# Linear attention and SiLU feed-forward on one core: opening outputs of each half of the heads in PSUM banks of their own, w_in loaded in 512-KB pieces through the pair ring, and two chunks' transposes issued ahead of later loads

## The chip, the cores and the metric

The kernel runs on one core of a Trainium2 chip. The metric is the device time of one execution in microseconds (us), lower is better. Each kernel was run several times, and medians are quoted with their range. The span, which the profile uses, is a little shorter than the device time: 212.7 us of 214.42 for the profiled run of the kernel before. The engines are called as the profile calls them: PE is the TensorE matmul, PEld its weight load, DVE is VectorE, ACT is ScalarE, POOL is GpSimd, and SP is the engine that issues the DMAs, whose queue appears as SPq.

## The reference

The computation has two parts. A causal linear attention with decay runs over 4 batches, 8 heads, 768 positions and head dimension 64. Its output, 3072 tokens of width 512, goes through a feed-forward network (FFN) with a SiLU.

```python
for b in range(nb):                                   # blocks of 64 positions
    sl = slice(b * block, (b + 1) * block)
    qb, kb, vb = (q[:, :, sl], k[:, :, sl], v[:, :, sl])
    intra = np.einsum('bhic,bhjc->bhij', qb, kb) * Dmask[None]
    intra = np.einsum('bhij,bhjd->bhid', intra, vb)
    inter = np.einsum('bhid,bhde->bhie', qb * lam_pow[None], kv_state)
    out[:, :, sl] = intra + inter
    kv_state = lam_block * kv_state + np.einsum('bhsd,bhse->bhde', kb * rev_pow, vb)
# ...
x = attn_out.transpose(0, 2, 1, 3).reshape(3072, 512)
h = x @ w_in                                          # 512 x 2048
out = (h / (1 + np.exp(-h))) @ w_out                  # 2048 x 512
```

## The kernel before

The kernel works in chunks of 128 tokens, 24 in all. Chunks are joined to groups of 256 or 384 tokens for the FFN. While the FFN of one group runs on the PE, the attention of the next group is woven in between. The start is special: chunks 0 to 3 (two pairs, "the opening") are written as an explicit list of small operations, because the PE has nothing else to do until weights have arrived.

For later chunks, POOL scales q and k (tiles `qb` and `kb`), SP issues a DMA transpose of each (`qt` and `kn`), and DVE spreads `kn` into a zero-padded tile `ktbd` (I call these the K copies). Only then can the PE compute the chunk's scores (`sp`).

Everything that SP issues, loads, transposes and stores, goes out in one order:

```python
def dma_t(c):
    qb, kb, vb = natb[c]
    # ... (tiles qt, kn)
    nc.sync.dma_start_transpose(qt, qb.rearrange("s p j d -> s (p j d)"))
    nc.sync.dma_start_transpose(kn, kb.rearrange("s p j d -> s (p j d)"))

def next_prep():
    c = state["prepped"]
    if c < NCHUNK:
        prep(c)                       # POOL: qb, kb
        if c >= NPET:
            dma_t(c)
        state["prepped"] = c + 1
        if loads:
            load_c(loads.pop(0))      # q, k, v of a later chunk, 256 KB each
# ... after the first groups' down-projections:
    st_d(5)
    next_prep()
    down0(3, 0)
    st_o(5)
    next_prep()
    clear_halves(0, 1)                # POOL: four memsets of ktbd and vpad
    down0(3, 1)
```

The opening leaves the tokens of groups 0 and 1 in a permuted order. Before the change a tile of 128 results holds every second token of the 256. The store of these four tiles therefore goes to every second row of the output:

```python
# op_x: attention outputs to the FFN's input, columns in the order (r, x, w)
move(e, xt[g].rearrange("d p (r x w) -> d p r x w", r=2, x=2)[:, ps, :, x, :], op_[c][:, ps])
# ...
# ffn2: result tile ob, 128 x 512
dst = out[r0:r0 + BLK, :]
if g < 2:
    dst = out[gstart[g]:gstart[g] + 256, :].rearrange("(q r) d -> q r d", r=2)[:, mt, :]
stores.append([0, dst, ob])           # issued later by nc.sync.dma_start(out=dst, in_=ob)
```

w_in is loaded in sixteen pieces of 256 KB into buffers that nothing else uses yet, and w_out in eight pieces of 512 KB through a ring of six buffers called `pair`. Each piece is then cast to bf16.

## Time and profile before

| what | before |
|---|---|
| time, median of 3 (range) | 215.58 us (214.94 to 215.84) |
| span of the profiled run | 212.7 us |
| PE busy | 204.5 us, 96% |
| first down-projection of the FFN | 33.59 us |
| longest PE wait after 22 us | 0.94 us, chunk 7's scores |

The first fence is from the page of the kernel before: the busy times of its first part, then busy tenths in 40 slices of 5.3 us each, the granted PE clock (the speed at which the PE was let run) in tenths of full speed (9 is 90% or more), and the DMA's share and rate.

```profile
PE 204.5 (96%) x1808; PEld 136.0 (64%) x1831; DVE 112.2 (53%) x263; ACT 98.4 (46%) x186; POOL 54.3 (26%) x66
...
PE   7979999999899999999999999999999999999994
...
PEclk9999999999999999999999999999999999999999
DMA  4999999998999997897999999889311011011112
GB/s 125 332 375 340 396 401 309 291 225 214 160 266 203 231 199 164 168 220 165 206 222 246 222 196 172 192 214 196 99 52 49 2 49 54 0 49 49 52 49 99
```

The PE is full except in the first slices. The DMA engines are over 90% busy from the second slice to the ninth and stay near it while chunks are being loaded, so the DMA has little slack either. The PE row counts 1808 matmuls and the PEld row 1831 weight loads. The records of 23 matmuls are missing from this trace.

The second fence is the view of the PE's waits before the change. Its columns are the total in us, how often, and the longest.

```profile
PE warm_ps L646 <- DVE zero L118: 1.1, 1, 1.1
PE sp L476 <- DVE ktbd L183: 0.9, 1, 0.9
PE kv_ps L641 <- ACT kvbd L179: 0.9, 1, 0.9
PE h_ps L529 <- ACT w_in_bf L179: 0.7, 1, 0.7
PE tk L270 <- POOL kp L253: 0.4, 1, 0.4
```

Only the 0.9 us for `ktbd` falls after the opening. The third fence is SP's timeline between 45 and 64 us, with start and length of each issue. `qt` and `kn` are the transposes of chunks 6, 7 and 8, and `out_dram<-ob` the stores.

```profile
46.93 1.21 SPq L374 DMA_TRANSPOSE kn<-kb  x1
...
50.61 1.18 SPq L570 DMA_DIRECT2D out_dram<-ob  x1
...
53.20 1.22 SPq L374 DMA_TRANSPOSE kn<-kb  x1
...
57.46 1.60 SPq L570 DMA_DIRECT2D out_dram<-ob  x3
59.23 1.24 SPq L373 DMA_TRANSPOSE qt<-qb  x1
60.56 1.21 SPq L374 DMA_TRANSPOSE kn<-kb  x1
61.82 0.57 SPq L232 DMA_DIRECT2D qf<-in_q_dram  x1
```

SP issues back to back.

The fourth fence is the view by windows of the kernel before. The columns are the window, its length, busy time (and count) of PE, PEld, DVE, ACT and POOL, granted clock, DMA share, and GB/s.

```profile
21.00:33.00 12.00, 11.54 (x106) 10.35 (x107) 5.81 (x12) 8.93 (x17) 0.00 (x0) 1.00 1.06 395
...
56.00:61.00 5.00, 4.00 (x45) 3.17 (x44) 3.67 (x10) 3.15 (x6) 2.14 (x2) 1.00 1.03 278
61.00:66.00 5.00, 5.00 (x38) 2.99 (x37) 2.63 (x9) 1.30 (x4) 0.60 (x1) 1.00 1.02 223
66.00:73.00 7.00, 6.95 (x76) 5.58 (x75) 4.51 (x11) 4.00 (x8) 3.03 (x4) 1.00 0.88 203
73.00:82.00 9.00, 8.90 (x94) 7.02 (x94) 7.48 (x18) 4.24 (x8) 2.70 (x3) 1.00 0.85 187
```

The last three permuted stores were issued from 57.46 us on and landed 3.6 to 3.7 us later. From 56 to 66 us, with other transfers in flight too, the DMA moves 278 and then 223 GB/s at a share of about 1, so on all of its 16 engines. (The share adds up the times of all packets, so it can pass 1; I read it only roughly.)

### The profile page before, as it was taken

Reading aid. Unit: us, or ns where it says so; the run is one execution under the profiler, and the core shown is the slowest. Engines: PE = TensorE matmul, PEld = TensorE weight load, DVE = VectorE, ACT = ScalarE, POOL = GpSimd, SP = SyncE. Lnnn points to the kernel's source line nnn. Section 1 sums busy time; section 2 is a strip of 40 time slices with the busy share of each in tenths; the row PEclk is TensorE's granted clock in tenths of the full one; section 3 lists DMA queues with packets and bytes.
Section 4 is the critical chain, followed back from the end, with each engine's and each line's share of the span. In section 5 each row is a group of like instructions: output and inputs, shape, how many; then the busy total and the mean of one; then the engine's idle time right before and its main releaser. Section 6 shows DMA issues by size and latency. Waiting matters only on the chain.

```text
span 212.7 us, 4591 instructions
## 1 busy us (share of the span) xinstructions
PE 204.5 (96%) x1808; PEld 136.0 (64%) x1831; DVE 112.2 (53%) x263; ACT 98.4 (46%) x186; POOL 54.3 (26%) x66
## 2 busy tenths in 40 slices
PE   7979999999899999999999999999999999999994
PEld 5667885567767877666665565556665565566654
DVE  3786458396766789555846975455561351110121
ACT  4983863415734554445554444444544344323210
POOL 6360004469333341313333432233000000000000
PEclk9999999999999999999999999999999999999999
DMA  4999999998999997897999999889311011011112
GB/s 125 332 375 340 396 401 309 291 225 214 160 266 203 231 199 164 168 220 165 206 222 246 222 196 172 192 214 196 99 52 49 2 49 54 0 49 49 52 49 99
DMA packets 95670, 38.58 MB, mean 181 GB/s; under 512 B 81056, under 2 KB 88608, under 8 KB 95648
## 3 DMA queue, kind: packets, MB, share of 16 engines
q1 hardware_dynamic: 95504, 38.29, 72.2%
q8 instruction: 14, 0.23, 0.5%
q14 instruction: 8, 0.07, 0.1%
q10 hardware_dynamic: 144, 0.00, 0.0%
HBM read 27.27 MB, written 6.29 MB: 158 GB/s over the span
## 4 chain that ended last, share of the span: by engine, by line
PE 71%; DMA 16%; SPq 9%; issue 1%; DVE 1%; POOL 1%; DVEq 0%
PE o_ps L578 30%; PE h_ps L552 20%; PE h_ps L529 11%; DMA pair<-in_moe_w_out_dram 4%; PE op L507 4%; SPq L224 4%; DMA qf<-in_q_dram 4%; SPq L232 3%; PE sp L476 3%; DMA vf<-in_moe_w_in_dram 3%; DMA qf<-in_moe_w_in_dram 3%; DMA kn<-kb 2%; PE o_part L595 2%; PE kv_ps L452 1%; SPq L161 1%
## 5 line engine op out<-in xcount | busy, mean ns | idle before, releaser
L578 PE MATMUL o_ps<-w_out_bf,g 128*128 128x512 bf16 x345 | 87.9, 379 | 1.2
L578 PEld LDWEIGHTS <-g 128*128 128x128 bf16 x368 | 35.0, 98 | 30.8
L556 ACT ACTIVATE g<-h_ps 128x384 bf16<-128x384 f32 x64 | 31.4, 490 | 46.7 <-PE h_ps L552 46.2
L552 PE MATMUL h_ps<-xt,w_in_bf 128*128 128x384 bf16 x256 | 50.6, 326 | 0.0
L529 PE MATMUL h_ps<-xt,w_in_bf 128*128 128x256 bf16 x384 | 47.2, 273 | 0.7 <-ACT w_in_bf L179 0.7
L534 ACT ACTIVATE g<-h_ps 128x512 bf16<-128x512 f32 x48 | 27.8, 596 | 32.4 <-PE h_ps L529 32.0
L529 PEld LDWEIGHTS <-w_in_bf 128*128 128x128 bf16 x384 | 36.4, 98 | 8.0 <-ACT w_in_bf L179 1.1
L582 DVE COPY ob<-o_ps 128x512 f32<-128x512 f32 x23 | 15.9, 691 | 41.1 <-PE o_ps L578 40.9
L356 POOL TENSOR_TENSOR qb<-qf,lam_fwd 128x512 bf16<-128x512 f32 x18 | 18.9, 1053 | 63.4 <-DMA qf<-in_q_dram 60.1
L552 PEld LDWEIGHTS <-w_in_bf 128*128 128x128 bf16 x256 | 23.7, 98 | 17.2
L483 DVE TENSOR_TENSOR ss<-sp,mask 128x512 bf16<-128x512 f32 (+1 forms) x40 | 21.0, 566 | 13.4 <-PE sp L476 13.0
L387 DVE COPY vpad<-vb 64x256 bf16<-64x256 bf16 x72 | 24.9, 346 | 1.6
L350 POOL TENSOR_TENSOR kb<-kf,lam_bwd 128x512 bf16<-128x512 f32 x20 | 21.7, 1086 | 4.4 <-DMA kf<-in_k_dram 4.0
L183 DVE CAST kvbd<-kv_ps 64x256 bf16<-64x256 f32 x32 | 13.5, 421 | 8.2 <-PE kv_ps L452 7.9
L515 ACT ACTIVATE xt<-op 128x512 bf16<-128x512 f32 x20 | 11.9, 597 | 12.7 <-PE op L507 12.0
L183 DVE COPY ktbd<-kn 64x512 bf16<-64x512 bf16 x36 | 10.6, 296 | 13.4 <-DMA kn<-kb 13.1
L476 PEld LDWEIGHTS <-ktbd 128*128 128x128 bf16 x160 | 9.4, 98 | 4.6 <-DVE ktbd L183 1.9
L476 PE MATMUL sp<-qt,ktbd 128*128 128x128 bf16 (+1 forms) x160 | 10.3, 207 | 0.9 <-DVE ktbd L183 0.9
L179 ACT ACTIVATE vb<-vf 128x512 bf16<-128x512 f32 x18 | 11.2, 622 | 0.0
L507 PE MATMUL op<-ss,vpad 128*128 128x128 bf16 (+1 forms) x160 | 10.3, 207 | 0.0
L507 PEld LDWEIGHTS <-vpad 128*128 128x128 bf16 x160 | 8.9, 98 | 0.3
L646 PE MATMUL warm_ps<-zero 128*128 128x256 bf16 x34 | 7.2, 387 | 1.1 <-DVE zero L118 1.1
(83 smaller groups left out, 119.6 us busy)
## 6 DMA issues: line engine op xcount, KB each, us to landing
out_dram<-ob SPq DMA_DIRECT2D x23, 256.0 KB, 3.4
kf<-in_k_dram SPq DMA_DIRECT2D x20, 256.0 KB, 4.2
vf<-in_v_dram SPq DMA_DIRECT2D x20, 256.0 KB, 4.3
qf<-in_q_dram SPq DMA_DIRECT2D x18, 256.0 KB, 3.5
pair<-in_moe_w_out_dram SPq DMA_DIRECT2D x8, 512.0 KB, 7.0
kf<-in_moe_w_in_dram SPq DMA_DIRECT2D x6, 256.0 KB, 5.5
vf<-in_moe_w_in_dram SPq DMA_DIRECT2D x6, 256.0 KB, 5.6
pair<-in_k_dram SPq DMA_DIRECT2D x4, 256.0 KB, 4.6
```

What stands on the lines that cost most here:

```text
L183: nc.vector.tensor_copy(dst, src)
L350: VG[e].tensor_tensor(kb, rawk.pop(c).rearrange("s (p j) d -> s p j d", j=2), decay(lam_bwd, c % NB), op=AL.mult)
L356: nc.gpsimd.tensor_tensor(qb, rawq.pop(c).rearrange("s (p j) d -> s p j d", j=2), decay(lam_fwd, c % NB), op=AL.mult)
L387: nc.vector.tensor_copy(vh[64 * j:64 * j + 64, :, h, j, :], vb[64 * h:64 * h + 64, :, j, :])
L476: nc.tensor.matmul(sp[:, p, :], lhsT=lhsT, rhs=qt[:, p, a:], start=True, stop=True)
L483: VG[e].tensor_tensor(ss, sp, m[:, None, :n].to_broadcast([128, 4, n]), op=AL.mult)
L507: nc.tensor.matmul(dst, lhsT=lhsT, rhs=rhs, start=(i == 0), stop=(i >= len(terms) - NP), skip_group_check=True)
L529: nc.tensor.matmul(hps[g, i][:, a:a + 256], lhsT=w_in_bf[:, ko, m * 128:(m + 1) * 128], rhs=xt[g][:, ko, :], start=(ko == 0 and u == 0), s ...
L534: nc.scalar.activation(gg.rearrange("p u n -> p (u n)"), hps[g, i], AF.Silu)
L552: nc.tensor.matmul(hp[:, a:z], lhsT=w_in_bf[:, ko, m * 128:(m + 1) * 128], rhs=xt[g][:, ko, a:z], start=(ko == 0 and a == 0), stop=(ko == ...
L556: nc.scalar.activation(gg, hp[:, :n], AF.Silu)
L578: nc.tensor.matmul(o, lhsT=gt[g, ko][:, mt * BLK:(mt + 1) * BLK], rhs=w_out_bf[:, ko, :], start=(ko == 0), stop=(ko == KO_OUT - 1))
```

## The change

The intent is to shorten the opening and to feed the chunks after it sooner. Each half of the heads gets PSUM banks of its own for the opening's outputs, so that one half's matmuls need not wait for the other half's eviction. The list of the opening is reordered, and 37 dummy matmuls go. w_in comes in eight loads of 512 KB through the `pair` ring, which makes fewer DMAs. The transposes of chunks 6 and 7 are issued together, ahead of the loads of chunks 8 and 9. Tiles are laid out with the half of the heads as an outer dimension. The FFN's input columns also change from (r, x, w) to (x, r, w), so the store of the first four result tiles gets another form.

```diff
-            if which == "in":
-                for a in range(2):
-                    # ... (256-KB pieces in the buffers of kf, vf and qf)
-            else:
-                # ... (w_out in pair)
+            ko, f = w_piece(which, i, 0, 2)
+            t = io.tile([128, 2, 512], F32, name="pair", tag="pair", bufs=6)
+            nc.sync.dma_start(out=t, in_=(w_in_r if which == "in" else w_out_r)[:, ko, f])
+            wtmp[which, i] = t
 # ... (ORDER rewritten; tiles [128, 2, H, D] become [128, 2, 2, 4, D])
 # op_o:
-        if a == 0:
-            for x, t in enumerate(tags):
-                op_[c + x] = psum.tile([128, NP, 2, 64], F32, name="op", tag=t, bufs=NBUF[t])
+        for x, t in enumerate(tags):
+            op_[c + x, a] = psum.tile([128, 2, 2, 64], F32, name="op", tag=t, bufs=NBUF[t], padded_shape=[128, NP, 2, 64])
 # op_x:
-            xt[g] = xpool.tile([128, KO_IN, GROUPS[g]], BF16, name="xt", tag="xt", padded_shape=[128, KO_IN, 512])
-        ps = slice(2 * a, 2 * a + 2)
-        move(e, xt[g].rearrange("d p (r x w) -> d p r x w", r=2, x=2)[:, ps, :, x, :], op_[c][:, ps])
+            t = xpool.tile([128, 2, KO_IN, BLK], BF16, name="xt", tag="xt", padded_shape=[128, 4, KO_IN, BLK])
+            xt[g] = t.rearrange("d x p n -> d p x n")
+        move(e, xt[g][:, 2 * a:2 * a + 2, x, :], op_[c, a].rearrange("d p r w -> d p (r w)"))
 # ffn2:
             if g < 2:
-                dst = out[gstart[g]:gstart[g] + 256, :].rearrange("(q r) d -> q r d", r=2)[:, mt, :]
+                dst = dst.rearrange("(w r) d -> r w d", r=2)
 # next_prep and its calls:
-    def next_prep():
+    def next_prep(load=1):
 # ...
-            if loads:
-                load_c(loads.pop(0))
+            for i in range(load):
+                if loads:
+                    load_c(loads.pop(0))
 # ...
-    next_prep()
+    next_prep(0)
+    next_prep(2)
     down0(3, 0)
     st_o(5)
-    next_prep()
     clear_halves(0, 1)
```

More of the change, by code (lines that the diff above doesn't have):

```diff
@@ L25 @@
 ORDER = """
-kc:0,0,A,u z:27 tk:0,0,att qc:0,0,D tq:0,0,h kc:0,1,D,s qt:0,0,D wl z:2 tk:0,1,att kt:0,1,A qc:0,1,P kt:0,0,D vc:0,0,D,s
-z:4 s:0,0,h,att m:0,0,0,D vc:0,1,A,u tq:0,1,o z:1 d:0 m:0,0,1,D qt:0,1,A z:2 s:0,1,att,att kc:2,0,P,s kv:0,A m:0,1,1,D
-m:0,1,0,D tk:2,0,h kt:2,0,D kc:2,1,A,u o:0,0,h,att qc:2,0,P qc:2,1,P x:0,0,A d:1 kv:1,A tq:2,0,o qt:2,0,D tk:2,1,o
-kt:2,1,D o:0,1 x:1,1,A z:3 tq:2,1,h qt:2,1,D vc:2,0,A,u vc:2,1,P,s s:2,0,att,o m:2,0,1,D z:4 s:2,1,o,att m:2,0,0,D
-m:2,1,1,D x:1,0,A m:2,1,0,D x:0,1,A w:0,1,D d:2 kv:2,A z:28 d:3 w:1,0,D o:2,0,o,att w:0,0,A o:2,1 x:2,0,D w:1,1,D w:2,0,D
-kv:3,A x:2,1,D u:0,0,0,h,h x:3,0,D x:3,1,A w:3,1,D w:2,1,A w:3,0,D u:0,0,1 w:6,0,D g:0,0,1 g:0,0,0 w:5,0,D w:4,1,A
-w:4,0,D u:1,1,0,o,o u:1,1,1 g:1,1,1 g:1,1,0 u:1,0,0,h,h u:1,0,1 g:1,0,0 g:1,0,1 w:7,0,D w:6,1,D w:5,1,A w:7,1,D
-u:0,1,0,o,o u:0,1,1 u:0,2,0,h,h g:0,1,1 u:0,2,1 g:0,1,0 u:0,3,0,o,o u:0,3,1 g:0,2,0 g:0,2,1 u:1,3,0,h,h g:0,3,0 g:0,3,1
-u:1,3,1 g:1,3,0 g:1,3,1 u:1,2,0,o,o u:1,2,1 g:1,2,1 g:1,2,0
+wl kc:0,0,D,u z:20 tk:0,0,att kt:0,0,A qc:0,0,D z:7 tq:0,0,att kc:0,1,D,s qc:0,1,P z:2 tk:0,1,o kt:0,1,A qt:0,0,D z:1
+s:0,0,h,o vc:0,0,D,s vc:0,1,A,u z:1 tq:0,1,o z:3 d:0 m:0,0,0,D kc:2,0,P,s qt:0,1,A s:0,1,h,att kv:0,A m:0,0,1,D qc:2,0,P
+m:0,1,0,D tk:2,0,att o:0,0,h,att kc:2,1,A,u x:0,0,A m:0,1,1,D d:1 tq:2,0,o kt:2,0,A o:0,1,h,o x:1,0,D qt:2,0,D qc:2,1,P
+tk:2,1,att x:1,1,A kv:1,A tq:2,1,h s:2,0,o,att vc:2,0,D,u vc:2,1,D,s kt:2,1,A qt:2,1,D m:2,0,1,D d:2 kv:2,A s:2,1,att,att
+m:2,0,0,D x:0,1,A w:0,1,D w:0,0,A m:2,1,1,D w:1,0,A d:3 o:2,0,att,o w:1,1,D x:2,0,D kv:3,A m:2,1,0,D x:3,0,A u:0,0,0,h,h
+u:0,0,1 g:0,0,1 o:2,1,att,att w:2,1,D w:2,0,D u:0,1,0,o,o w:3,0,D w:3,1,A u:0,1,1 g:0,0,0 x:3,1,D x:2,1,A g:0,1,1
+u:1,1,0,h,h u:1,1,1 w:4,0,D w:5,1,D g:0,1,0 w:6,1,D w:6,0,D w:7,0,D g:1,1,0 u:1,0,0,o,o w:7,1,D g:1,1,1 u:1,0,1 w:4,1,A
+g:1,0,0 u:0,3,0,h,h g:1,0,1 u:0,3,1 u:1,3,0,o,o g:0,3,1 w:5,0,D u:1,3,1 g:0,3,0 g:1,3,1 g:1,3,0 u:0,2,0,h,h u:0,2,1
+g:0,2,1 u:1,2,0,o,o g:0,2,0 u:1,2,1 g:1,2,0 g:1,2,1
 """
@@ L154, in load_w @@
         for i in pieces:
-            if which == "in":
-                for a in range(2):
-                    ko, f = w_piece(which, i, a, a + 1)
-                    n = 2 * i + a
-                    tag = "qf" if n >= 12 else ("kf", "vf")[a]
-                    t = io.tile([128, 1, 512], F32, name=tag, tag=tag, bufs=4 if tag == "qf" else 6)
-                    nc.sync.dma_start(out=t, in_=w_in_r[:, ko, f])
-                    wtmp[which, i, a] = t
-            else:
-                ko, f = w_piece(which, i, 0, 2)
-                t = io.tile([128, 2, 512], F32, name="pair", tag="pair", bufs=6)
-                nc.sync.dma_start(out=t, in_=w_out_r[:, ko, f])
-                wtmp[which, i] = t
+            ko, f = w_piece(which, i, 0, 2)
+            t = io.tile([128, 2, 512], F32, name="pair", tag="pair", bufs=6)
+            nc.sync.dma_start(out=t, in_=(w_in_r if which == "in" else w_out_r)[:, ko, f])
+            wtmp[which, i] = t
     def cast_w(which, i, e="D", part=None):
@@ L171, in cast_w @@
         ko, f = w_piece(which, i, a, b)
-        if which == "in":
-            move(e, w_in_bf[:, ko, f], wtmp[which, i, part])
-        else:
-            move(e, w_out_bf[:, ko, f], wtmp[which, i][:, a:b, :])
+        move(e, (w_in_bf if which == "in" else w_out_bf)[:, ko, f], wtmp[which, i][:, a:b, :])
     def move(e, dst, src):
@@ L206, with zeros @@
     cell = {}
+    def zeros(dst):
+        for i in range(cell.pop("z", 0)):
+            nc.tensor.matmul(dst, lhsT=zero[:, :BLK], rhs=zero, start=True, stop=True, skip_group_check=True)
     start = 0
@@ L247, in pair_op @@
         hs = slice(4 * a, 4 * a + 4)
-        src, dst = src[:, hs].rearrange("s h r d -> s r h d"), dst[:, :, hs, :]
+        src, dst = src[:, hs].rearrange("s h r d -> s r h d"), dst[:, a]
         if table is None:
@@ L259, in run @@
             if c not in tiles:
-                tiles[c] = nat.tile([128, 2, H, D], BF16, name=name, tag=name, bufs=2)
+                tiles[c] = nat.tile([128, 2, 2, 4, D], BF16, name=name, tag=name, bufs=2)
             pair_op(c, a, e, lam_fwd if forward else lam_bwd if s == "s" else None, raw[c], tiles[c])
@@ L268, in run @@
                 for p in range(2):
-                    h = 4 * a + 2 * p
-                    nc.tensor.transpose(tp[:, r, p, :], src[c][:, r, h:h + 2, :], ident)
+                    nc.tensor.transpose(tp[:, p, r, :], src[c][:, a, r, 2 * p:2 * p + 2, :], ident)
             cell[name, c, a] = tp
@@ L276, in run @@
             if c not in dst:
-                dst[c] = nat.tile([128, 2, NP, BLK], BF16, name=name, tag=name, bufs=2)
-            move(e, dst[c][:, :, 2 * a:2 * a + 2], cell.pop((of, c, a)))
+                dst[c] = nat.tile([128, NP, 2, BLK], BF16, name=name, tag=name, bufs=2)
+            move(e, dst[c][:, 2 * a:2 * a + 2], cell.pop((of, c, a)))
         return run
@@ L284, in op_s @@
         sps = [psum.tile([128, 2, 2, 2, 64], F32, name="sp", tag=t, bufs=NBUF[t]) for t in tags]
+        zeros(sps[0][:, 0])
         for r in range(2):
@@ L287, in op_s @@
                 for j, x in ((0, 0), (1, 1), (0, 1), (1, 0)):
-                    nc.tensor.matmul(sps[j][half[x], r, p], lhsT=ktp[c][half[j], r, 2 * a + p, half[x]],
-                                     rhs=qtp[c][half[j], :, 2 * a + p, half[x]], start=True, stop=True)
+                    nc.tensor.matmul(sps[j][half[x], r, p], lhsT=ktp[c][half[j], 2 * a + p, r, half[x]],
+                                     rhs=qtp[c][half[j], 2 * a + p, :, half[x]], start=True, stop=True)
         sp_[c, a] = sps
@@ L298, in op_o @@
     def op_o(c, a, *tags):
-        if a == 0:
-            for x, t in enumerate(tags):
-                op_[c + x] = psum.tile([128, NP, 2, 64], F32, name="op", tag=t, bufs=NBUF[t])
+        for x, t in enumerate(tags):
+            op_[c + x, a] = psum.tile([128, 2, 2, 64], F32, name="op", tag=t, bufs=NBUF[t], padded_shape=[128, NP, 2, 64])
+        zeros(op_[c, a])
         for x in range(2):
@@ L304, in op_o @@
                 for p in range(2):
-                    nc.tensor.matmul(op_[c + x][:, 2 * a + p], lhsT=kvb[c + x][:, 2 * a + p, :],
-                                     rhs=qtp[c][:, :, 2 * a + p, half[x]], start=(a == 0 and p == 0),
-                                     stop=False, skip_group_check=True)
+                    nc.tensor.matmul(op_[c + x, a][:, p], lhsT=kvb[c + x][:, 2 * a + p, :],
+                                     rhs=qtp[c][:, 2 * a + p, :, half[x]], start=(p == 0), stop=False, skip_group_check=True)
         for r in range(2):
@@ L310, in op_o @@
                 for x, j in ((0, 0), (1, 1), (0, 1), (1, 0)):
-                    nc.tensor.matmul(op_[c + x][half[j], 2 * a + p], lhsT=vp[c][half[x], r, 4 * a + 2 * p + j, :],
-                                     rhs=ss_[c, a, j][half[x], r, p], start=(c + x == 0 and a == 0 and r == 0 and p == 0),
+                    nc.tensor.matmul(op_[c + x, a][half[j], p], lhsT=vp[c][half[x], a, r, 2 * p + j, :],
+                                     rhs=ss_[c, a, j][half[x], r, p], start=(c + x == 0 and r == 0 and p == 0),
                                      stop=(r == 1), skip_group_check=True)
@@ L329, in op_d @@
                 for j in range(2):
-                    nc.tensor.matmul(kv[half[j], p, half[j]], lhsT=kp[c0][half[x], r, 2 * p + j, :],
-                                     rhs=vp[c0][half[x], r, 2 * p + j, :], start=(c == 0 and r == 0 and p == 0), stop=True,
+                    nc.tensor.matmul(kv[half[j], p, half[j]], lhsT=kp[c0][half[x], p // 2, r, 2 * (p % 2) + j, :],
+                                     rhs=vp[c0][half[x], p // 2, r, 2 * (p % 2) + j, :], start=(c == 0 and r == 0 and p == 0), stop=True,
                                      skip_group_check=True)
@@ L628, in op_u @@
             ffn1_open(g, i, tag)
+        if h == 0:
+            zeros(hps[g, 2 * b][:, 0:256])
         for i in (2 * b, 2 * b + 1):
@@ L639, in op_z @@
         if 0 in kvps:
-            for i in range(n):
-                nc.tensor.matmul(kvps[0][half[0], NP - 1, half[1]], lhsT=zero[:, half[0]], rhs=zero[:, half[0]],
-                                 start=False, stop=True, skip_group_check=True)
+            cell["z"] = n
         else:
```

## The prediction

> **What bounds the kernel now.** By the page's first part the PE is busy 204.5 of 212.7 us; the granted clock is 0.998. The waits of the PE sum to about 4 us, and only three fall after real work began: 0.9 us for the kv copies (15.9 us), 0.7 us for a w_in cast (21.5) and 0.94 us for chunk 7's K transpose (58.0). Busy is not useful, though. The PE's timeline shows 27 dummy matmuls up to 6.9 us, then the opening (attention of chunks 0 to 3) stretched over 6.9 to 18.6 us. Adding its matmuls at their dense durations (four transposes about 0.23 us, sixteen 64-column ones about 0.33) gives some 6.5 us of work in those 11.7 us. The FFN runs without a break only from 21.46. So at most 6 to 7 us can be recovered; the first load lands at about 5.0 us and cannot come sooner.
>
> **What the change does.**
> 1. Each half of the heads gets its own PSUM bank for the opening outputs. Before, the second half's first matmul (12.47) began only after the first half's eviction (11.91 + 0.38 us). The Trainium skill, "PSUM — Partial Sum Buffer", section Terms, says that TensorE and another engine on one bank and quadrant at once collide; this agrees with the wait seen. Worth some tenths, twice.
> 2. The order: 37 dummy matmuls after the first state update go (about 1.9 us, mostly filling idle time). The FFN's first half-pieces come before the last output of chunk pair 2. The Trainium skill, "TensorE: Matmul & The Clock Gate", Part 1, needs about 3.4 us of idleness to fall to half rate; the dummies show that rate (0.22 us for 256 columns) until about 7 us; no gap here is that long, so the clock stays.
> 3. w_in in eight 512-KB loads through the six pair buffers. They now wait for casts, but 4 to 6 us of transfers are in flight, and the DMA is full from 5 to 45 us (windows view). I expect arrivals unchanged within 0.5 us: W0 near 15.8, W7 near 25.5.
> 4. Chunk 7's transposes move ahead of load 8 and a store: its K transpose issues near 49.5 instead of 53.2 and lands near 53 instead of 57.3.
>
> **On the critical path.** Walking the new order by hand with these durations: transposes and scores of chunk pair 2 are no earlier (14 to 15.5 us), but the FFN starts near 17 and runs without gaps from about 21, with 12 half-pieces of 0.88 us left instead of 14. First down-projection near 32.3 instead of 33.6: 1.3 us gained, plus the 0.94 us stall: about 2.3 us. Not all may last. The sync queue issues transposes, loads and stores back to back from 45 us, about 6.2 us per chunk; the K spreads end only 0.05 to 0.8 us before the PE wants chunks 9, 12, 13 and 14. That queue gains perhaps 1 us; a PE that is further ahead will stall there.
>
> **Predicted: 213.6 us, 211.8 to 215.2.** Faster by over 2%: 0.07; within 2%: 0.91; slower: 0.02.
>
> **What would show it.** First down-projection at 31.5 to 33; no PE wait before chunk 7's scores; new waits of tenths at chunks 9, 12, 14 for K spreads released by a DMA; the PE's busy time down 2 to 3 us (dummies gone); steady durations unchanged (0.216 us for 512 columns); the second half's output matmuls no longer behind the eviction.
>
> **What would make it wrong.** The w_in ring starves the DMA (W7 after 27 us): slower. The sync queue gains nothing: then the gain is near zero. The queue's pace follows the PE more than I read (stores, buffers), so the full opening gain lasts, or the opening gains 3 us or more: below 211.8.

## The result, and the profile after

| what | before | after |
|---|---|---|
| time, median of 4 (range) | 215.49 us (214.94 to 215.84) | 235.16 us (234.63 to 236.29) |
| span of the profiled run | 212.7 us | 232.9 us |
| PE busy | 204.5 us, 96% | 207.2 us, 89% |
| mean granted clock | 0.998 | 0.971 |
| first down-projection | 33.59 us | 32.80 us |
| scores of chunks 6, 7 and 8 start | 52.50, 58.01, 66.08 us | 54.06, 60.40, 83.53 us |

The kernel became 9.2% slower: the ratio is 1.0922, with a 95% interval of 1.0873 to 1.0971. A run is called slow when it is over 1.5% above the fastest of its kernel, and fast otherwise; the four runs after are marked fast, and the four before lie within 0.5% of each other. A ratio in this text is of fast runs alone, so it is not quite the ratio of the medians quoted beside it. The result lies far outside the predicted range of 211.8 to 215.2 us.

The page after the change, in slices of 5.8 us, shows the PE empty from 70 to 82 us. The DMA row falls to one tenth in the slice before that, and the GB/s row reads 51, 71 and 53 from 64 to 82 us:

```profile
PE 207.2 (89%) x1794; PEld 134.6 (58%) x1794; DVE 121.5 (52%) x263; ACT 99.3 (43%) x187; POOL 53.3 (23%) x65
...
PE   8889999996870069998999999999999999999995
...
PEclk9999999999998559999999999999999999999999
DMA  5999999979415999899999999973931100111112
GB/s 144 336 361 355 350 322 329 261 146 212 114 51 71 53 221 208 181 190 220 225 183 225 226 205 203 229 180 91 190 83 45 49 26 19 46 48 45 45 48 90
```

The PE's waits after the change put nearly all of it on one line, the scores that wait for the K copies:

```profile
PE sp L467 <- DVE ktbd L171: 17.6, 3, 14.9
```

The PE's timeline after the change shows the three of them (chunks 6, 7 and 8) and what followed. In brackets stand the wait and its releaser.

```profile
54.06 0.51 PE L467 MATMUL sp<-qt,ktbd 128*128 128x128 bf16 x8 [1.66 <-DVE ktbd L171]
54.41 1.91 PE L520 MATMUL h_ps<-xt,w_in_bf 128*128 128x256 bf16 x16
...
60.40 0.51 PE L467 MATMUL sp<-qt,ktbd 128*128 128x128 bf16 x8 [1.08 <-DVE ktbd L171]
...
83.53 0.80 PE L467 MATMUL sp<-qt,ktbd 128*128 128x128 bf16 x8 [14.89 <-DVE ktbd L171]
84.14 3.41 PE L520 MATMUL h_ps<-xt,w_in_bf 128*128 128x256 bf16 x16
```

DVE's K copies are only the last link. DVE itself had waited 18.89 us for `kn<-kb`, the DMA:

```profile
82.79 0.59 DVE L171 COPY ktbd<-kn 64x512 bf16<-64x512 bf16 x2 [18.89 <-DMA kn<-kb]
```

SP's timeline after the change shows why that DMA came late. The lines are chunk 7's K transpose, then the four permuted stores, then chunk 8's transposes.

```profile
51.20 1.22 SPq L365 DMA_TRANSPOSE kn<-kb  x1
...
57.89 8.34 SPq L561 DMA_DIRECT2D out_dram<-ob  x4
66.43 9.46 SPq L364 DMA_TRANSPOSE qt<-qb  x1
76.00 2.46 SPq L365 DMA_TRANSPOSE kn<-kb  x1
```

The stores took 8.34 us to issue, and the `qt` transpose behind them took 9.46 us to issue and landed 15.8 us after its issue began, at 82.2 us; `kn` landed at 82.7. Before, the same `qt` issue took 1.24 us. The view by windows of the kernel after tells what the DMA did meanwhile:

```profile
21.00:33.00 12.00, 11.79 (x105) 9.95 (x105) 5.44 (x12) 8.12 (x16) 0.00 (x0) 1.00 0.96 328
...
61.00:66.00 5.00, 5.00 (x45) 3.40 (x43) 2.82 (x6) 1.79 (x3) 0.75 (x1) 1.00 0.15 51
66.00:73.00 7.00, 2.63 (x17) 1.37 (x14) 0.00 (x0) 1.11 (x2) 0.00 (x0) 1.00 0.13 51
73.00:82.00 9.00, 0.00 (x0) 0.00 (x0) 0.00 (x0) 0.00 (x0) 0.00 (x0) 0.53 1.12 76
```

From 61 to 73 us the DMA moved a steady 51 GB/s at a share of 0.13, where it had moved 203 to 223 GB/s. After a burst in each of the windows 74 to 75 and 77 to 78 us it was back at 51 GB/s, until 81 us. Only then did chunk 8's transposes land. A share of 0.13 is 2 of 16 engines (2/16 = 0.125). The store's access pattern says 2 as well: the new form of the destination is 2 x 64 x 512, the old one 128 x 512. At 51 GB/s the four stores of 256 KB need about 1,049 KB / 51 GB/s = 20.6 us, an estimate from these two numbers; the stretch at 51 GB/s lasts from about 61 to 81 us.

The Trainium skill, "DMA: Bandwidth & Descriptors", section "Why a DMA increments its semaphore by 16 and not by 1", states the rule that fits. The number of engines k is the largest one up to 16 that divides the slowest dimension (not of size 1) of both access patterns, "as the instruction carries it". Here that is 2. This trace agrees with it (0.13 of the engines). The prediction had not looked it up.

The sum works out so. Chunk 8's scores came at 83.53 us instead of 66.08, that is 17.45 us late. Of these, 14.89 are the wait itself and 2.56 had been lost before it. Then the clock was at half until about 87.2 us, which cost about 1.8 us (estimated from a window of 85 to 88 us with a mean clock of 0.63: half clock for 2.2 of its 3 us, and so for 3.7 us from 83.53). Some 1 us of the 20.2 us by which the span grew is spread over the rest.

### The profile page after: what moved, and what is told of

The parts are those of the page before. It is cut to its first block, busy times and chain, and to the rows that moved or that the text cites. A ratio compares the mean times of both kernels' runs of the same rounds, so it can differ in the third digit from the quotient of the medians.

```text
span 232.9 us, 4538 instructions
## 1 busy us (share of the span) xinstructions
PE 207.2 (89%) x1794; PEld 134.6 (58%) x1794; DVE 121.5 (52%) x263; ACT 99.3 (43%) x187; POOL 53.3 (23%) x65
## 4 chain that ended last, share of the span: by engine, by line
PE 58%; DMA 21%; SPq 8%; DVE 7%; POOL 2%; issue 2%; ACT 1%; POOLq 0%; DVEq 0%
PE o_ps L569 26%; PE h_ps L543 18%; DMA pair<-in_moe_w_out_dram 8%; PE h_ps L520 6%; DMA kn<-kb 5%; SPq L364 4%; PE op L498 3%; DMA qf<-in_q_dram 3%; PE sp L467 3%; DMA pair<-in_moe_w_in_dram 2%; DVE vpad L378 2%; DVE ktbd L171 2%; DMA pair<-in_k_dram 2%; SPq L216 2%; SPq L561 2%
## 5 line engine op out<-in xcount | busy, mean ns | idle before, releaser
L569 PE MATMUL o_ps<-w_out_bf,g 128*128 128x512 bf16 x368 | 91.7, 379 | 0.0
L520 PE MATMUL h_ps<-xt,w_in_bf 128*128 128x256 bf16 x384 | 49.3, 278 | 0.8 <-DVE w_in_bf L171 0.6
L474 DVE TENSOR_TENSOR ss<-sp,mask 128x512 bf16<-128x512 f32 (+1 forms) x40 | 21.0, 566 | 15.8 <-PE sp L467 15.5
L378 DVE COPY vpad<-vb 64x256 bf16<-64x256 bf16 x72 | 27.7, 385 | 1.6
L171 DVE COPY ktbd<-kn 64x512 bf16<-64x512 bf16 x36 | 15.9, 443 | 20.2 <-DMA kn<-kb 19.8
L637 PE MATMUL warm_ps<-zero 128*128 128x256 bf16 x34 | 6.7, 357 | 1.1 <-DVE zero L118 1.1
```

Of the source, the lines that this page charges most:

```text
L171: nc.vector.tensor_copy(dst, src)
L378: nc.vector.tensor_copy(vh[64 * j:64 * j + 64, :, h, j, :], vb[64 * h:64 * h + 64, :, j, :])
L474: VG[e].tensor_tensor(ss, sp, m[:, None, :n].to_broadcast([128, 4, n]), op=AL.mult)
L520: nc.tensor.matmul(hps[g, i][:, a:a + 256], lhsT=w_in_bf[:, ko, m * 128:(m + 1) * 128], rhs=xt[g][:, ko, :], start=(ko == 0 and u == 0), s ...
L569: nc.tensor.matmul(o, lhsT=gt[g, ko][:, mt * BLK:(mt + 1) * BLK], rhs=w_out_bf[:, ko, :], start=(ko == 0), stop=(ko == KO_OUT - 1))
```

## The experiments

The theory was that the form of the store alone makes the loss. The rivals were the w_in ring, the transposes issued ahead and the new opening. A second question came up on the way: when the store is mended, why is the kernel still not faster, although its opening is? Eighteen kernels were run, in five jobs; each job had its own runs of the kernel before. "ch6" is chunk 6, and so on. The times are medians of all runs, slow ones included (e8, e11, e14, e15 and e16 have some).

| run | what it is | time, us | before, us | ratio (95%) |
|---|---|---|---|---|
| e1 | after, each permuted store split in two | 221.02 | 215.37 | 1.0264 (1.0225 to 1.0303) |
| e2 | after, old column order and store | 218.54 | 215.37 | 1.0133 (1.0100 to 1.0167) |
| e3 | before, store with outer dimension 2 | 234.27 | 215.37 | 1.0879 (1.0839 to 1.0920) |
| e4 | e1, old order of transposes | 219.12 | 215.37 | 1.0185 (1.0153 to 1.0217) |
| e5 | e2, old w_in loads | 217.37 | 215.91 | 1.0050 (0.9968 to 1.0132) |
| e6 | e5, old order of transposes | 217.54 | 215.91 | 1.0066 (0.9973 to 1.0158) |
| e7 | before, transposes ahead | 216.99 | 215.91 | 1.0027 (0.9941 to 1.0114) |
| e8 | before, w_in ring | 217.95 | 215.91 | 0.9992 (0.9866 to 1.0117) |
| e9 | e5, q and k of ch6 and ch7 loaded early | 220.67 | 215.06 | 1.0275 (1.0226 to 1.0325) |
| e10 | e7, the same early loads | 219.94 | 215.06 | 1.0221 (1.0173 to 1.0269) |
| e11 | e9, POOL's memsets later | 224.88 | 215.06 | 1.0412 (1.0345 to 1.0479) |
| e12 | before, store with outer dimension 8 | 217.17 | 215.06 | one run |
| e13 | e5, memsets on DVE and later | 215.80 | 215.43 | 1.0019 (0.9972 to 1.0065) |
| e14 | before, memsets on DVE and later | 217.17 | 215.43 | 1.0060 (1.0007 to 1.0113) |
| e15 | e13, loads and casts rearranged | 218.61 | 215.43 | 1.0116 (1.0064 to 1.0168) |
| e16 | e6, memsets on DVE and later | 219.67 | 215.43 | 1.0170 (1.0122 to 1.0219) |
| e17 | e13, memsets later still | 216.12 | 216.18 | 1.0030 (0.9986 to 1.0075) |
| e18 | e7, memsets as in e17 | 216.39 | 216.18 | 1.0023 (0.9973 to 1.0073) |

### The store: e1, e2, e3, e12

e1 keeps the whole change and issues each permuted store as two stores of 64 rows.

```diff
-            nc.sync.dma_start(out=dst, in_=ob)
+            if len(dst.shape) == 3:
+                for r in range(2):
+                    nc.sync.dma_start(out=dst[r], in_=ob[64 * r:64 * r + 64, :])
+            else:
+                nc.sync.dma_start(out=dst, in_=ob)
```

> The kernel after, with one edit: each store of the first two groups, whose address pattern has an outer dimension of 2 (rows r, then 64 rows w), is issued as two stores of 64 rows. Theory A (the 2-outer stores run on 2 of the 16 DMA engines: share 0.13 and 51 GB/s from 61 to 82 us, 1 MB in about 20 us, and chunk 8's transposes queue behind them): the stretch at 51 GB/s is gone, the 14.9 us wait at chunk 8 is gone, PE clock stays 1.0 near 80 us, time 214 to 218 us. Rival B (two chunks' transposes back to back, with both loads behind them, hold up the queue): the store's form is indifferent, time stays 232 to 237. Rival C (the w_in ring delays every later load): also unchanged, 232 to 237.

It took 221.02 us. The wait of 14.9 us was gone, and with it 14 us of the time. The expectation was too low by some 3 us: the first down-projection came at 33.91 us, 1.1 later than in the kernel after, whose opening it shares, shorter waits for K copies stayed (2.27 us at ch6, 1.21 at ch7, 1.83 at 83.31 us), and the eight half stores still took SP 6.26 us to issue.

e2 keeps the change except for the column order, and so has the old store.

```diff
-            t = xpool.tile([128, 2, KO_IN, BLK], BF16, name="xt", tag="xt", padded_shape=[128, 4, KO_IN, BLK])
-            xt[g] = t.rearrange("d x p n -> d p x n")
-        move(e, xt[g][:, 2 * a:2 * a + 2, x, :], op_[c, a].rearrange("d p r w -> d p (r w)"))
+            xt[g] = xpool.tile([128, KO_IN, GROUPS[g]], BF16, name="xt", tag="xt", padded_shape=[128, KO_IN, 512])
+        ps = slice(2 * a, 2 * a + 2)
+        move(e, xt[g].rearrange("d p (r x w) -> d p r x w", r=2, x=2)[:, ps, :, x, :], op_[c, a])
 # ...
-                dst = dst.rearrange("(w r) d -> r w d", r=2)
+                dst = out[gstart[g]:gstart[g] + 256, :].rearrange("(q r) d -> q r d", r=2)[:, mt, :]
```

> The kernel after, with the token order of the first two groups in xt put back (columns r, x, w instead of x, r, w), and with it the old store of 128 rows at a stride of two rows; everything else of the change stays. Theory A: 214 to 218 us, within 1 us of e1_split and perhaps a little faster, because it issues four stores fewer. Rivals B and C: 232 to 237 us.

It took 218.54 us: of the loss of 9.2%, 7.9 points are gone. It is also 1.1% below e1 of the same job. Its four stores of 128 rows took SP 3.00 us to issue, against 6.26 for the eight of 64. But the two kernels also differ in the column order, and e2's first down-projection came 0.59 us sooner, so the 1.1% is not shown to be the stores'.

e3 is the other way round: the kernel before with nothing but an outer dimension of 2 on these stores. The rows land in the wrong order; bytes and count stay as they were.

```diff
                 dst = out[gstart[g]:gstart[g] + 256, :].rearrange("(q r) d -> q r d", r=2)[:, mt, :]
+                dst = dst.rearrange("(w a) d -> a w d", a=2)
```

> The kernel before with only the four stores of the first two groups given an outer dimension of 2 (even rows, then odd rows of the block: the rows land permuted, so 512 output rows are wrong on purpose). Theory A: the DMA falls to about 51 GB/s and a share of 0.13 for about 20 us, chunk 8's or 9's K transpose lands 10 to 17 us late, PE stalls that long, time 226 to 236 us. Rivals B and C: no w_in ring and no transposes ahead, so 214 to 217 us.

It took 234.27 us (ratio 1.0879), nearly all of the change's 1.0922. The window of e3's trace from 66 to 73 us has the same signature:

```profile
66.00:73.00 7.00, 6.34 (x45) 3.63 (x44) 0.90 (x3) 2.31 (x4) 0.00 (x0) 1.00 0.13 51
```

The waits split in two here (5.07 us at ch7 and 9.91 at ch8), because the first store goes out before ch7's transposes when these aren't issued ahead. So the loss needs none of the other parts of the change.

e12 is e3 with `a=8` in place of `a=2`, to see whether it is the count that matters or any third dimension at all.

> e3 with an outer dimension of 8 instead of 2 in the four stores (512 output rows permuted, wrong on purpose). Theory A as a law (the outer dimension is the number of engines): each engine moved about 25.6 GB/s with 2, so 8 engines move about 205 GB/s, 1 MB in 5 us instead of 20, and the DMA share of a stretch with only stores is near 0.5; time 215 to 219 us. If the form of the pattern matters and not the count, it stays 226 or more.

One look gave 217.17 us. The windows of 1 us while these stores were in flight read:

```profile
61.00:62.00 1.00, 1.00 (x8) 0.52 (x7) 0.94 (x4) 0.60 (x1) 0.00 (x0) 1.00 0.52 162
62.00:63.00 1.00, 1.00 (x16) 0.76 (x15) 0.99 (x4) 0.29 (x1) 0.00 (x0) 1.00 0.51 161
```

A share of 0.52 is 8 of 16. So the number of engines follows the outer dimension: 2 gave 0.13, 8 gave 0.52, 128 gave about 1 (in traffic mixed with loads). The rate was below the expected 205 GB/s: about 20 GB/s per engine (162/8), against 25.5 (51/2) with two engines. What limits it there is not known.

### The order of the transposes, the ring and the opening: e4 to e8

e4 is e1 with the old order of transposes and loads (`next_prep()` after `st_d(5)` and after `st_o(5)`, as before the change).

> e1_split with the old order of transposes and loads (chunk 6's transposes, load 8, chunk 7's transposes, load 9). Theory A with my prediction's step 4: the chunk 7 wait of about 1 us grows to 2 to 4 us, because chunk 7's K transpose is issued about 4 us later; time 0.5 to 3 us above e1_split. Rival B: if having the transposes ahead is what hurts, this is at least 2 us faster than e1_split.

It took 219.12 us, 1.9 us *less* than e1. The expectation was the opposite. Issuing the transposes ahead did not pay here; why it cost as much as 1.9 us was not settled.

e5 is e2 with the old w_in loads instead of the ring.

> e2_oldrows with the w_in loads put back as well (16 loads of 256 KB in their own buffers, no ring). Theory D (the ring makes w_in and w_out loads wait for casts, the DMA moves 333 instead of 395 GB/s between 21 and 33 us, and chunk 6's transposes issue at 47.7 to 49.3 instead of 45.3 to 46.9 us, which is the 1.9 us wait at chunk 6): 325 GB/s becomes 380 or more in that stretch, the chunk 6 wait falls below 0.7 us, time 1.5 to 3 us under e2_oldrows, so 215.5 to 217. Rival E (the waits at chunks 6 to 8 come from having both chunks' transposes and the POOL memsets close together, not from late loads): the wait at chunk 6 stays over 1.2 us and time within 0.7 us of e2_oldrows.

It took 217.37 us, level with the kernel before (1.0050, interval across 1). Its first down-projection came at 32.41 us, 1.2 us earlier than before. By ch6 this was lost: a wait of 1.43 us, with the two K copies taking 2.48 us while POOL's memsets ran. Neither of its theories came out whole: 362 GB/s and this wait speak against D, and a ratio 0.8 points below e2's speaks against E.

e6 is e5 with the old order of transposes too, so that of the change only the opening (order, banks, layouts) remains.

> The kernel before with only the new order of the opening, the banks per half and the tile layouts inside the opening: old store, old w_in loads, old order of transposes and loads. My prediction's opening gain alone (about 1 us at the first down-projection) would give 213 to 215 us if the later queue does not take it back; with the queue taking it back at chunks 7, 9 and 12, as predicted, 214.5 to 216. If the new order itself is worse (rival F), over 216.5.

217.54 us: in the range set for rival F, but level with before, which took 215.91 us in that job. First down-projection at 32.38 us, then a wait of 2.33 us at ch6, with K copies of 3.33 us under the memsets.

e7 is the kernel before with only the transposes ahead.

> The kernel before with only the transposes of chunks 6 and 7 ahead of loads 8 and 9. As predicted: the 0.94 us wait at chunk 7 goes, time 214 to 215.5 us (0 to 1 us faster). If e4 against e1 (1.9 us in favour of the old order) holds here too: 216 to 218 us, with new waits at chunk 8 or later because loads 8 and 9 start about 3 us later.

216.99 us, level with before. ch7's wait fell from 0.94 to 0.33 us as intended. But ch6 now waited 1.01 us, with K copies of 2.05 us, because POOL's memsets ran later. They stand behind the scaling of chunk 7's q, which started at 47.46 us instead of 46.29, when that q arrived. The order of the loads up to that q is the same in both kernels, so this delay may be one of that run and not of the edit.

e8 is the kernel before with only the ring.

> The kernel before with only the w_in loads in 512-KB pieces through the six pair buffers. Theory D: the w_out loads issue over 7 to 9 us instead of 3.5, GB/s between 21 and 33 us falls from 395 to below 350, chunk 6's K transpose issues 1 us or more later, a wait of 0.5 to 2 us appears at chunk 6 or 7; time 216 to 218 us. As I predicted it (arrivals within 0.5 us): 215 to 216 us, no new wait.

The time is inconclusive: two of its four runs, the profiled one among them, were slow, and the two fast ones lie 2.3 us apart (214.97 and 217.27). But what the ring does to the loading can be read from the window of 21 to 33 us of the fast traces that share the new opening. Four with the old w_in loads (e5, e6, e13, e17) have 362 to 394 GB/s there, mean 376. Four with the ring (after, e1, e2, e4) have 323 to 336, mean 330. Chunk 6's K transpose was issued at 47.29 to 49.34 us in the first set and at 48.59 to 49.59 in the second: 1.0 us later in the mean, though the ranges overlap. The pieces of w_in themselves came as predicted in the kernel after: the casts of W0 began at 15.74 us (15.8 predicted) and the cast that waited for W7 at 25.96 (25.5 predicted). What came behind them was late. The first six w_out loads took 8.95 us to issue instead of 3.49, and SP's waits from 9 to 30 us put 5.4 us, in six waits, down to DVE's casts of w_in, which free the ring's buffers (the profile infers who ended a wait).

### K copies against POOL's memsets: e9 to e16

e9 tries to have K early: q and k of chunks 6 and 7 are loaded before the last w_out pieces and v.

```diff
     load_k(4), load_k(5)
+    for c in (6, 7):
+        rawq[c] = load_1(q, c, "qf", 4)
+        load_k(c)
     load_w("out", 6, 7)
     load_v(4), load_v(5)
-    load_c(6)
-    load_c(7)
+    load_v(6), load_v(7)
```

> e5_oldrows_oldw with the q and k loads of chunks 6 and 7 moved ahead of the last two w_out loads and of the v loads of chunks 4 to 7. Theory G (after the stores are mended, what takes back the opening's gain is that q and k of chunks 6 and 7 arrive at 43 to 49 us, because the DMA is full from 5 to 45 us, so that the K spreads are late): chunk 6's K transpose issues at 44.5 us or earlier instead of 48.2, the waits at chunks 6, 7 and 8 together fall from 3 us to below 1 us, time 212.5 to 214.8 us. If the transposes' own pace or the PE's work limits instead: 215.5 to 217.5.

It failed, with 220.67 us. The last w_out piece now lands later, and its cast on ACT stands before chunk 4's `qt` copies in ACT's order: the PE waited 3.91 us at chunk 4. But it told something: K of ch6 had landed long before, and ch6 still waited 0.98 us, with copies that took 2.02 us while POOL scaled q and k (56.28 to 58.37 us).

e10 makes the same early loads in e7.

> e7 (before, with the transposes of chunks 6 and 7 ahead) with the same early q and k loads. Theory G: no wait over 0.4 us at chunks 6 and 7, but the opening stays as before, so the first down-projection stays near 33.5 and the time is 214 to 215.5, 1 us or so above e9. If e9 is not below this one, the new opening brings nothing even when the loads are early.

219.94 us, and the same fault: a wait of 4.66 us for ACT. e9 is not below it, but with this fault in both, the pair doesn't tell what the new opening is worth.

e11 moves POOL's memsets of e9 to the middle of the next group's up-projections, to take them off the K copies of ch6.

```diff
-    clear_halves(0, 1)
     down0(3, 1)
 # ...
+    ([(clear_halves, 0, 1)], 0.5, 0.5),      # in the list of the next group's stretch
```

> e9 with the four POOL memsets of the buffers of chunks 4 and 5 moved from before the group to its middle. Theory H (DVE copies of bf16 stand still while POOL works: the two K copies of chunk 6 took 2.63 us together in the kernel after, with the memsets at the same time, against 0.78 in the kernel before): the two K copies of chunk 6 take about 0.6 to 0.8 us, and the wait there is at least 0.5 us below e9's if e9 still has it. If the copies still take over 1.5 us, something else slows them. Time between e9 minus 1 and e9 plus 0.5.

It took 224.88 us (two of six runs slow; the profiled one is slow, but its memsets take 0.95 us each as in the fast traces). It put the memsets exactly on top of the copies. Below are the two K copies on DVE's timeline, and then POOL's timeline of the same stretch of e11:

```profile
57.44 4.87 DVE L183 COPY ktbd<-kn 64x512 bf16<-64x512 bf16 x2
...
57.49 0.95 POOL L198 MEMSET ktbd<- 128x1024 bf16 x1
58.38 0.95 POOL L199 MEMSET vpad<- 128x1024 bf16 x1
59.27 0.95 POOL L198 MEMSET ktbd<- 128x1024 bf16 x1
60.16 0.95 POOL L199 MEMSET vpad<- 128x1024 bf16 x1
```

Two copies that take 0.59 us when POOL is idle took 4.87 us. The Trainium skill, "SBUF — State Buffer", section "Who interferes with whom", says that DVE's copies in a two-port mode and GpSimd need the same pair of ports, and that the loser is blocked altogether. The trace agrees. The same collision stands, smaller, in the kernel after. Its K copies of ch6 on DVE and its memsets on POOL:

```profile
51.38 2.63 DVE L171 COPY ktbd<-kn 64x512 bf16<-64x512 bf16 x2
...
49.94 0.95 POOL L186 MEMSET ktbd<- 128x1024 bf16 x1
50.82 0.95 POOL L187 MEMSET vpad<- 128x1024 bf16 x1
51.72 0.95 POOL L186 MEMSET ktbd<- 128x1024 bf16 x1
52.61 0.95 POOL L187 MEMSET vpad<- 128x1024 bf16 x1
```

Before the change the memsets ran from 48.27 to 51.89 us, and the same two copies, at 51.57, took 0.78 us:

```profile
51.57 0.78 DVE L183 COPY ktbd<-kn 64x512 bf16<-64x512 bf16 x2
```

Only the tail of the last memset met them. After, POOL began on chunk 7's q at 47.95 us instead of 46.29 (it waited for that load), its memsets ended at 53.56, and the copies met them in full.

e13 takes the memsets off POOL: e5 with the memsets on DVE, in the middle of the next group.

```diff
-            nc.gpsimd.memset(ktbd[i], 0.0)
-            nc.gpsimd.memset(vpad[i], 0.0)
+            nc.vector.memset(ktbd[i], 0.0)
+            nc.vector.memset(vpad[i], 0.0)
 # ... and the call moved as in e11
```

> e5_oldrows_oldw with the four memsets of the buffers of chunks 4 and 5 done by DVE in the middle of the next group instead of by POOL before it. Theory H: chunk 6's two K copies take 0.6 to 0.8 us instead of 2.48, the wait at chunk 6 (1.43 us in e5) falls below 0.5 us, and the ratio to before falls from 1.005 to 0.994 to 1.000. Rival I (late loads alone): the copies may be quick, but the wait at chunk 6 or 7 stays within 0.5 us of e5's sum (2.9 us) and the ratio stays at 1.003 or more.

215.80 us (1.0019). The copies of ch6 took 0.59 us, and ch6 no longer waited: its scores started at 51.33 us, 1.2 before those of the kernel before. So POOL's memsets were the cause of ch6's wait. But now the memsets on DVE (54.88 to 56.98 us) stood in front of ch7's copies, and ch7 waited 1.75 us. The ratio just missed the expected 0.994 to 1.000.

e14 is the control: the kernel before with the memsets moved the same way.

> The control: the kernel before with only the memsets moved to DVE. In it POOL's memsets ended at 51.9 us, as the copies began, so theory H expects nothing or little: ratio 0.994 to 1.001, chunk 7's wait as before (about 0.9 us).

217.17 us (1.0060), above the expected 0.994 to 1.001. Its profiled run was slow (clock 0.977), so its waits are not compared.

e15 rearranges the loads and casts in e13 once more: k and q of ch6 before the last w_out loads, those of ch7 after, v of both later, and the last w_out casts behind the chunk 5 copies.

> e13 with q and k of chunk 6 loaded ahead of the last two w_out loads, q and k of chunk 7 right behind them, the v loads of chunks 6 and 7 behind chunk 6's transposes, and the last two w_out casts behind the copies of chunks 4 and 5. Theory I: chunk 6's K transpose issues by 45.5 us and chunk 7's by 50, no wait over 0.5 us at chunks 6 and 7, time 1 us or more below e13, ratio 0.985 to 0.993. If H alone was the matter, within 0.5 us of e13. A wait for a w_out or v cast of more than 1 us would spoil it, as in e9.

218.61 us (1.0116), a failure: other casts, now of v on ACT, came late (2.63 us at chunk 4's state, in a trace that is slow).

e16 is e6 with the memsets on DVE.

> e6_order_banks_only (new order and banks, old stores, w_in loads and transposes order) with the memsets on DVE. Theory H: chunk 6's copies 0.6 to 0.8 us instead of 3.33, its wait below 0.8 us instead of 2.3. Against e13 it tells what the two chunks' transposes ahead are worth: by my prediction's step 4, e13 is faster by 0.5 to 1 us, with the wait at chunk 7 under 0.5 us there and over 1 us here.

Its verdict is unclear by the 2% rule (1.0170); one run was far off at 242.34 us with a clock of 0.854, and the profile fell on that one, so its waits are not compared. But its five fast runs took 218.19 to 220.55 us, and e13, which differs only in issuing the transposes ahead, took 215.09 to 217.75 in the same job. So here the transposes ahead gain about 3 us, where 0.5 to 1 was expected, while in e4 against e1 they cost 1.9 us.

### Where the opening's gain ends: e17 and e18

e17 is e13 with the memsets still later, behind ch7's masks and its output. e18 is the control: the old opening with the same memsets and the same order of transposes.

```diff
-    ([(clear_halves, 0, 1)], 0.5, 0.5),
+    ([(clear_halves, 0)], 0.8, 0.8), ([(clear_halves, 1)], 1.2, 1.2),
```

> e13 with the two buffers' memsets on DVE after the masks of chunk 7 and, for the second buffer, after its output, so that they stand ahead of no K copy of chunks 6 and 7. Theory H: both chunks' copies take about 0.6 us, waits at chunks 6 and 7 together below 0.7 us instead of 1.75 (e13) and 2.9 (e5), ratio to before 0.990 to 0.998. If the ratio is still 1.000 or more although those waits are gone, the opening's gain is taken back later, at chunks 9 to 14, as I had predicted of the sync queue.

> The control for the opening: the kernel before with the transposes of chunks 6 and 7 ahead and the same memsets, but the old opening. First down-projection at 33.5 to 33.7 us. If the opening's gain lasts, e17 is faster than this by 0.5 to 1.3 us; if it is taken back later, the two are within 0.4 us.

e17 took 216.12 us and e18 216.39, and in the same job the kernel before took 216.18: no difference that these runs can show. Yet e17's opening is 1.1 us faster (first down-projection 32.50 against 33.59 before), and its ch7 scores started at 56.53 us, 1.5 ahead of those before. Then this lead went. The PE's timeline of e17 at ch8, and DVE's copies just before it:

```profile
66.22 0.51 PE L479 MATMUL sp<-qt,ktbd 128*128 128x128 bf16 x8 [1.46 <-DVE ktbd L183]
...
65.58 0.59 DVE L183 COPY ktbd<-kn 64x512 bf16<-64x512 bf16 x2 [4.55 <-DMA kn<-kb]
```

Against that stands the same chunk in the kernel before:

```profile
66.08 0.50 PE L476 MATMUL sp<-qt,ktbd 128*128 128x128 bf16 x8
```

A PE that comes 1.5 us sooner waits 1.46 us for the transposed K of ch8, and starts at 66.22 instead of 66.08. ch12 waits another 0.83 us. DVE had been idle for 4.55 us, so it is the DMA and not the copies. The new order of the transposes has a part in this: chunk 8's K transpose was issued at 62.10 us in e17 and at 60.56 before, and its K copies began at 65.58 and 63.44 us. At the times of the kernel before, the copies end at 64.03 us, 2.05 us ahead of the scores, so a PE 1.5 us ahead would not have waited there (worked out, not tested). So no version here beats the kernel before.

## Why the prediction was wrong

1. **The step that failed is the account of the sync queue, "That queue gains perhaps 1 us": it left out the store.** The prediction's "What the change does" has four items, and none is the store; the line `dst.rearrange("(w r) d -> r w d", r=2)` was passed over. It left 2 of 16 DMA engines to four stores: 51 GB/s, about 20 us of transfer, a wait of 14.89 us at ch8 and half clock after it. e3 shows that this effect alone makes a ratio of 1.0879, where the whole change makes 1.0922; e1 and e2 show that without it the wait of 14.9 us is gone; e12 shows that the engines follow the count. That chunk 8's transposes queue behind the stores' data on those two engines is argued from the order, the shares and their landing at 82.2 and 82.7 us, just after the stretch at 51 GB/s. The traces show only that they wait, and that they don't when the stores run on 16.

2. **The opening: right in sign and near in size without the ring, not with it.** The prediction had the first down-projection at 32.3 us (31.5 to 33), and it came at 32.80; the FFN started at 16.45 us (near 17 predicted, 18.60 before). Without the ring the first down-projection came at 32.38 to 32.52 in five fast traces (e5, e6, e9, e13, e17), so the new opening gains about 1.1 us of the 1.3 predicted. With the ring it was 32.80 to 33.91 in four (after, e1, e2, e4), against 33.59 before. So 32.80 is the best of four, and that it fell within the range is partly luck. As for the banks: the second half's output matmuls began at 12.11 us, 0.05 before the first half's eviction ended, and no longer after it. But before the change the PE didn't wait there: its transposes filled the time up to 12.47. What the banks are worth by themselves, no run shows. The prediction leaned there on the Trainium skill, "PSUM — Partial Sum Buffer", section Terms, on collisions; no run here tests it.

3. **The ring: right for w_in, wrong for what loads behind it.** "Arrivals unchanged within 0.5 us" held in the kernel after for the pieces it named (W7 at 25.96 us against 25.5), though W7 came at 26.49 in e2. But the window of 21 to 33 us moved 330 instead of 376 GB/s, and chunk 6's K transpose was issued 1.0 us later in the mean. The prediction had looked at bytes in flight and not at the later loads that queue behind a ring which waits for casts. That it waits for casts is what SP's waits say (5.4 us, releaser inferred); no run tests it.

4. **The transposes ahead did not do what was said.** Chunk 7's K transpose was predicted to issue near 49.5 us and did at 51.20, and "no PE wait before chunk 7's scores" became 1.08 us. A wait nobody had listed appeared a chunk earlier: 1.66 us at ch6, because POOL's memsets moved onto the K copies. e11 and e13 show that cause. The order has no one price: it is worth nothing measurable in e7 (1.0027), it cost 1.9 us in e1 against e4, and it gained about 3 us in e13 against e16. The waits of tenths that were forecast at chunks 9, 12 and 14 don't appear in the kernel after, where the PE waited for K only at 6, 7 and 8.

5. **"A PE that is further ahead will stall there" came true, partly by luck.** e17 keeps the lead as far as ch7 and loses it at ch8 and ch12 to transposes. The prediction had named chunks 9, 12, 13 and 14, and at ch8 the new order itself had made the transposes later; e17 and e18, with and without the new opening, end within 0.3 us of each other. Even with a harmless store the change would have been no gain; the prediction of 213.6 us had let about 2 us of it last.

6. **PE busy down 2 to 3 us: not readable as predicted.** It rose from 204.5 to 207.2 us. But 23 matmul records are missing before: the `o_ps` group is listed with 345 matmuls and 87.9 us there, with 368 and 91.7 after. And half clock lengthened the group of 256-column `h_ps` matmuls from 47.2 to 49.3 us. Taking off these 3.8 and 2.1 us leaves 201.3, or 3.2 below. The weight loads, 1831 and 1794, show that the 37 dummies are gone. Also the prediction's "so the clock stays" held for the opening, of which it was said, and fell at the hole of 14.9 us.

The clock fits the Trainium skill, "TensorE: Matmul & The Clock Gate", Part 1, by which an idle PE falls to half rate after an idle window of about 3.4 us, and the windows run freely, so that the fall can come later than 3.4 us after the stop. Here the PE stopped at 68.64 us, and the granted clock was 1.00 up to 73 us, 0.78 in 73 to 74 and 0.50 in 74 to 75. It fell at about 73.6 us, some 4.9 us after the stop. In e3, by the same reading, it fell 4.8 and 3.7 us after its two stops. Sixteen matmuls of 256 columns took 3.41 us afterwards, and 1.91 us at full clock.

What stays open: what the ring alone costs in time (e8 inconclusive), why the order of the transposes costs 1.9 us in one pair of kernels and gains 3 in another, why the opening is slower and less steady with the ring, and what the banks alone are worth.

## What to carry to other kernels

Read every changed access pattern of a DMA for its outermost dimension before reading anything else of a diff: a `rearrange` that puts a 2 in front moves the same bytes at an eighth of the engines, and whatever is issued behind it on the same queue pays. Splitting it by hand helps (e1); keeping 128 partitions outermost and permuting elsewhere halved the time of issue here (e2, 3.00 against 6.26 us). A faster opening is worth only what the next shared resource lets through, so follow the lead chunk by chunk until it meets the next wait, and when instructions on POOL move in time, look at which DVE copies they now fall upon.

## What the Trainium skill lacked or had wrong

- "DMA: Bandwidth & Descriptors" has the rule for the number of engines and it held (shares of 0.13, 0.52 and about 1 for outer dimensions of 2, 8 and 128). Its rate for one engine names no direction; for these SBUF-to-HBM stores it was here 25.5 GB/s each with two engines (51 GB/s) and about 20 each with eight (162 GB/s).
- The same page, "Rules for kernel authors", warns that a small outermost dimension confines that DMA. It gives no figure for what this costs the DMAs behind it on the same issuing engine: a transpose there took 9.46 us to issue instead of 1.24 and landed after 15.8 us, with 14 of the 16 engines unused for 12 us.
- The same section says of two transfers to disjoint halves of the partitions that they serialize, and gives no cost of issuing them. Eight stores of 64 rows here took 6.26 us to issue (e1), four of 128 rows 3.00 us (e2).
- "SBUF — State Buffer", section "Who interferes with whom", says that the first to issue holds the shared ports for the whole instruction. It doesn't say how often a blocked copy can lose: with POOL's instructions back to back, one DVE copy out of two took 3.82 us, across four memsets of 0.95 us each (e11, slow).
- "TensorE: Matmul & The Clock Gate", Part 1, was right within what the traces resolve: half clock 4.9 us (after), 4.8 and 3.7 us (e3) after the PE stopped.
